# Four sums moved to GpSimd, second value products in halves, and a new order of sums and value copies in a fused attention and SwiGLU kernel

## The chip, the core and the metric

The kernel runs as one program on one core of a Trainium2 chip. The metric is the device time of one execution in microseconds (us); less is better. The times given are medians of runs.

## What is computed

Softmax attention for 8 batches of 12 heads, 448 tokens each, head size 64. Its output, seen as 3584 tokens of width 768, goes through a gated feed-forward network of inner width 1536:

```python
scores = matmul(q, k.transpose(0, 1, 3, 2)) / sqrt(64)
attn = exp(scores - max(scores)); attn = attn / (sum(attn) + 1e-09)
x = matmul(attn, v).transpose(0, 2, 1, 3).reshape(3584, 768)
g = x @ w_gate                                   # 768 -> 1536
out = (g * sigmoid(g) * (x @ w_val)) @ w_out     # 1536 -> 768
```

All inputs and the output are float32; the kernel works on float16 copies and accumulates in float32.

## The kernel before, in words

**Attention.** Two heads make a pair; there are 48 pairs, numbered 0 to 47. A pair's scores come from `qk` (lines 327, 339, 357), ScalarE takes their exponentials into `E` (lines 347, 365), and the product with the values accumulates in `acc` (lines 383, 391, 418). VectorE closes a pair with a reciprocal and a multiplication (lines 402 and 404 for the first twelve pairs, 447 and 448 for the others) into `xt`, which is then transposed into `X`, the input of the feed-forward part (lines 483 and 490 by TensorE and VectorE, 492 and 496 by DMA). Before a pair's value product can start, VectorE copies its values from the landing place `vraw` to `vo` (`copy_v`, line 218). The loads into `vraw` are issued by GpSimd (lines 177, 211). For the first six pairs the list `CAT` says behind which score unit each copy stands in VectorE's queue: entry 2 is pair 2, entry 3 is pair 3. `XAT` does the same for the transposes.

**Feed-forward, first half.** Every two batches (896 tokens) are cut into two blocks; a *block* of 384 or 512 tokens is worked off in 12 *steps*, one for each 128 of the 1536 inner columns. A step has a gate product (`gate`, tile `gp`), a tanh on ScalarE (`sg`, line 582), `t = (sg + 1) * gp` on VectorE (`gated`, line 608), a value product (`value`, tile `vp`) and `hts = t * vp` on VectorE (`close`, line 614). Both products are six matmuls of line 555. `run_pair` runs two steps together: gate one, gate two, value one, value two. Where a step has `split`, its value product is made in two halves of the tokens, each followed by its own `close`; the first half goes to `spare`, the unused second bank of the first step's gate tile. In the kernel before, the second step of a pair is split when the block is 512 tokens wide and the pair is not in a place marked `gate_small`.

**PSUM.** The pool `ps_s` has three tiles of two banks (scores, gates, the groups `og`, the units `un`), the pool `ps_f` two tiles of one bank (`acc`, `vp`, `op`, `ub`). A tile's next user waits until the last reader of the former one is done.

**Feed-forward, second half.** Part of it is plain (`op`, line 648, 12 matmuls of 192 columns). The rest goes by `out_group` (line 677), which needs seven products instead of eight for two blocks of 128 tokens, and for that needs sums made beforehand: `out_sums` (lines 527 to 530) over the weights, and `h_sums` (lines 538 to 541) over `hts`: `s3 = a11 - a21`, then `a21 = a21 + a22` in place, `s2 = a21 - a11`, `s4 = a12 - s2`. All of these are VectorE instructions on 128x768 float16. They wait in the list `sums`; `add_sum` issues the next one.

**Order.** The order of the instructions of each engine is the order of the calls. The list `VISITS` says for each visit of the main loop how many steps, groups, plain outputs and sums are issued; its last number is the number of sums. `FIRST_STEPS` does so for the seven visits before it. In the last three visits block 4 (384 tokens), the last in-line block, is waiting for its output groups; its four `h_sums` are issued there.

**The end.** After the loop, block 5 (512 tokens in two halves of 256) is made by `Unit`: 12 units of seven products (`un`, `ub`, line 793) between which ScalarE and VectorE combine (lines 835, 839, 842, 846, 858, 860). Units 0 and 1 begin with a small matmul `Z` (line 830) into a bank of `ps_f`. The units need sums of the weights, made by GpSimd (`weight_sums`, lines 756 to 759, four instructions of 128x384 float16 each; `W_6` to `W_11` in the list of items). `order_of` plans the order of all items from costs given by hand. Behind the units come one plain output (`O`), block 4's groups, block 5's groups, then the last block in the same way with 448 tokens.

Of the kernel before, what the change touches and what calls it, by code (L numbers as in the profile page):

```python
# [38 lines left out]
PE_, ACT_, DVE_, POOL_ = "PE", "ACT", "DVE", "POOL"  # L39
# [25 lines left out]
def kernel(  # L65
# [10 lines left out]
    nc = tc.nc  # L76
# [6 lines left out]
    NFB = DF // 128  # L83
# [66 lines left out]
    def hview(lo, n):  # L150
        return hall[:, ds(lo * NFB, n * NFB)].rearrange("p (f t) -> p f t", t=n)
# [64 lines left out]
    def copy_v(pr):  # L216
        m = 128 if pr >= QUAD else P
        nc.vector.tensor_copy(Vts[pr % NV][0:m, :, :, 0:D], vraw[0:m, pr % VS])
# [299 lines left out]
    gate_small = [False]  # L518
# [11 lines left out]
            lambda: nc.vector.tensor_sub(t4, b21, t2),  # L530
        ]

    def h_sums(hts, t, at):
        lo, hi, x, y = slice(0, NH), slice(NH, NFB), ts(2 * t, 128), ts(2 * t + 1, 128)
        a11, a12, a21, a22 = hts[:, lo, x], hts[:, hi, x], hts[:, lo, y], hts[:, hi, y]
        s2, s3, s4 = Hall[at]
        return [
            lambda: nc.vector.tensor_sub(s3, a11, a21),
            lambda: nc.vector.tensor_add(a21, a21, a22),
            lambda: nc.vector.tensor_sub(s2, a21, a11),  # L540
            lambda: nc.vector.tensor_sub(s4, a12, s2),
        ]

    class Step:
# [337 lines left out]
    with tc.manual_schedule():  # L882
# [33 lines left out]
        def emit(item):  # L916
            if item[0] == "qk":
                load_qk16(*item[1:])
            elif item[0] == "V":
                load_v(item[1] * GP, GP)  # L920
            else:
                load_w(*item)
# [8 lines left out]
        sums = []  # L931
# [14 lines left out]
        def add_block(i, visits):  # L946
            if i < B - NB - 1:
                f1, own, n = block(i)
                fvq.extend(f1)
                kk, c0, hts = own  # L950
            else:
                own = None
            t_out = NFB * OH / 2400.0
            if i == 0:
                oq.extend([(ffn2_steps(*own, by_half(range(n // 128), OH)), t_out)] * (2 * (n // 128)))
            if i < 2:
                if i:
                    ffn2_wait.append(own)
                    sums.extend(wsums)
                    wsums.clear()  # L960
                return
            kk, c0, hts = ffn2_wait.pop()
            ffn2_wait.append(own)
            odd = i % 2 == 0
            groups.extend(x for t in range(1 + odd) for x in pair_groups(kk, c0, hts, t))
            if not odd:
                w = QW
                oq.extend([(ffn2_steps(kk, c0, hts, by_half([2], w)), t_out)] * (DM // w))
            sums.extend(groups[0][1])
            later = [f for _, fs in groups[1:] for f in fs]  # L970
            groups[:] = [(begin, []) for begin, _ in groups]
            sums.extend(later)
# [11 lines left out]
        ]  # L984

        def token_sums(x, w, t, eng=nc.vector):
# [22 lines left out]
        def add_sum(n=1):  # L1009
            for _ in range(n):  # L1010
                if sums:
                    sums.pop(0)()

        def run_fv(quiet=False):
            step = fvq.pop(0)
            step.gate()
            step.value(0)
            if not quiet:
                add_sum()
            step.finish()  # L1020
            if not quiet:
                add_sum()
            return 2 * step.time

        def run_pair(small=0):
            one, two = fvq.pop(0), fvq.pop(0)
            two.split = two.at[2] == 512 and not gate_small[0]
            one.gate()
            two.gate()
            two.spare = one.spare  # L1030
            one.value(0)
            one.gated()
            if small == 1:
                add_sum()
            two.gated()
            one.finish()
            two.value(0)
            if not small:
                add_sum()
            two.finish()  # L1040
            if small == 2:
                add_sum()
            return 4 * one.time

        def run_single():
# [14 lines left out]
        def run_o():  # L1060
            gen, t = oq.pop(0)
            next(gen)
            if len(oq) < 2 and not groups and wsums:
                n = 3 if oq else 4
                sums.extend(wsums[:n])
                wsums[:n] = []
                add_sum(n)
            return t
# [38 lines left out]
        def run_budget(budget):  # L1107
            while (fvq or oq) and budget > 0:
                if not fvq:
                    budget -= run_o()  # L1110
                elif len(fvq) > 1 and fvq[0].at[1] and 2 * fvq[0].time < budget <= 4 * fvq[0].time:
                    budget -= run_pair(2)
                else:
                    budget -= run_fv(bool(fvq[0].at[1]))
            return budget

        def left():
            return sum(2 * step.time for step in fvq) + sum(t for _, t in oq)
# [2 lines left out]
            return (at + 1) * total // n - at * total // n  # L1121

        XAT = (10, 14, 17, 21)
        CAT = (3, 7, 11, 14, 17, 21)
        pieces = [(p, c) for p in range(FIRST) for c in range(NC)]

        def piece():
# [2 lines left out]
        for u in range(FIRST * NC):  # L1130
# [12 lines left out]
            if c == 1:  # L1143
                for w in wq.pop(pr, []):
                    emit(w)
            if u in CAT:
                copy_v(CAT.index(u))
            if u in XAT:
# [42 lines left out]
        def bare_next(x):  # L1191
            return x + 1 < len(plan) and not plan[x + 1][1]
# [9 lines left out]
        for x, (chunks, todo) in enumerate(plan):  # L1202
# [54 lines left out]
            if 0 < base - x <= len(FIRST_STEPS):  # L1257
                n = FIRST_STEPS[x - base]
                gate_small[0] = bare
                if n > 1:  # L1260
                    run_pair(1)
                else:
                    run_fv(True)
            elif x < base:
                if bare and oq and not fvq:
                    carry -= run_o()
                elif bare:
                    gate_small[0] = True
                out_small[0] = not fvq and bool(oq) and any(p0 >= QUAD for _, p0 in todo)
                extra = 2 * fvq[0].time if bare and len(chunks) == 3 and fvq and not fvq[0].at[1] else 0  # L1270
                carry = run_budget(left() / (end - x) + carry + extra) - extra
            else:
                begins, nf, ng, no, ns = VISITS[x - base]
                gate_small[0] = bare
                if begins > 2:
                    add_block(begins, 0)
                after_group = ng > 0
                out_small[0] = bool(no) and not bare
                if around:
                    run_group_with(todo[0][1])  # L1280
                elif ng:
                    run_group(nf, gate_first=bare)
                    nf = 0
                if bare_next(x):
                    for _ in range(nf):
                        run_fv()
                else:
                    run_steps(nf)
                for _ in range(no):
                    run_o()  # L1290
                    out_small[0] = True
                out_small[0] = False
                if begins == 2:
                    add_block(2, 0)
                ahead = {3: (x + 1, x + 2), 2: (), 1: ()}.get(len(VISITS) + base - x, (x + 1,))
                for p0 in [p for y in ahead for p in vcopies.get(y, [])]:
                    copy_v(p0)
                add_sum(ns)
                if x == len(VISITS) + base - 6:
                    space = raws_all[:, 0 : RL // 2].rearrange("p a t b x -> p (a t b x)")  # L1300
                    wsum_space(space, 10)
                    for _ in range(3):
                        wsum_space(attp.tile([128, 4 * NC * D], FP16, tag="qk16", name="wsum", bufs=3), 2)
                    wsum_space(Eall, 4)
                    wsum_space(vfree, 4)
# [60 lines left out]
        items = unit_items(units, lambda u: Unit(u, 256, x5, t5, hts5), 256)  # L1366
# [13 lines left out]
        for m, fn in enumerate(groups5[0][0][1]):  # L1380
            u = NFB - 1 if m else NH - 1
            items[f"H{m}"] = (DVE_, 0.6, [f"F00_{u}", f"F10_{u}"] + [f"H{m - 1}"] * (m > 0), fn)

        items["O"] = (PE_, 1.0, [f"P{n}_{NFB - 1}" for n in (2, 3, 4)], run_o)
        run_items(items)

# [18 lines left out]
        hts = hview(0, NT)  # L1405
        units = {}
        items = unit_items(units, lambda u: Unit(u, S, x7, t7, hts), S)
# [51 lines left out]
```

## Time and profile before

| | |
|---|---|
| median of 3 runs | 436.31 us (435.48 to 436.58) |
| profiled execution | 436.53 us, of it 434.8 us span |
| TensorE (PE) busy | 423.5 us, 97% of the span |
| VectorE (DVE) busy | 272.4 us, 63% |
| ScalarE (ACT) busy | 245.5 us, 56% |
| GpSimd (POOL) busy | 226.7 us, 52% |
| granted TensorE clock | 1.0 of full speed, throughout |

"PE s L327" is the TensorE instruction of line 327 that writes the tile `s`. In the timeline each row has the start in us, the time from the first start to the last end, the engine, the line, output and inputs, shapes and number of instructions; what stands in brackets is how long the engine had been idle before, and what ended that. Ends of matmuls are modelled: consecutive rows of PE overlap by the length of the pipeline, so distances between starts tell more than busy times. "PEld" is the weight load in front of a matmul.

### The profile page before, as it was taken

What the parts mean: (1) busy time and instruction counts of PE and PEld (TensorE: products, weight loads), DVE (VectorE), ACT (ScalarE), POOL (GpSimd) and SP (SyncE); (2) the same over time, 40 slices, a digit from 0 to 9 for tenths busy, and PEclk for the clock granted to TensorE, in tenths of its full rate; (3) what the DMA queues carried; (4) which work ended last, traced back from release to release, by engine and by line L of the source; (5) the groups of instructions that cost most, each with busy time, mean ns of one, the idle gap of its engine ahead of it and who ended that gap; (6) DMA issues with size and microseconds to landing.
All of it is one profiled execution on the core that took longest, in us unless ns stands there. A gap on an engine that the chain in (4) does not pass through costs nothing.

```text
span 434.8 us, 11461 instructions
## 1 busy us (share of the span) xinstructions
PE 423.5 (97%) x4564; PEld 284.5 (65%) x4564; DVE 272.4 (63%) x634; ACT 245.5 (56%) x395; POOL 226.7 (52%) x350
## 2 busy tenths in 40 slices
PE   8999999999999999999999999999899999999996
PEld 3665666645456667747665677776688995555795
DVE  4666652785668556565635776678777655575663
ACT  6875667646656655656666546668454225545221
POOL 8755723998795774647743875926992000000001
PEclk9999999999999999999999999999999999999999
DMA  9999999999999999999889999623100322000124
GB/s 133 191 199 200 198 168 177 137 170 218 141 132 144 117 165 116 133 137 125 117 127 134 166 125 100 138 54 95 23 2 3 110 83 64 0 2 0 38 75 146
DMA packets 108550, 50.01 MB, mean 115 GB/s; under 512 B 60864, under 2 KB 105232, under 8 KB 108496
## 3 DMA queue, kind: packets, MB, share of 16 engines
q0 software_dynamic: 46944, 24.83, 52.0%
q1 hardware_dynamic: 61408, 24.27, 31.0%
q8 instruction: 36, 0.59, 0.6%
q14 instruction: 18, 0.15, 0.2%
q10 hardware_dynamic: 144, 0.17, 0.1%
HBM read 49.55 MB, written 11.01 MB: 139 GB/s over the span
## 4 chain that ended last, share of the span: by engine, by line
PE 85%; DVE 9%; ACT 3%; issue 2%; DVEq 0%
PE og L677 17%; PE gp L555 14%; PE vp L555 12%; PE un L793 9%; PE ub L793 7%; PE acc L418 7%; PE s L327 4%; PE op L648 3%; PE s L357 2%; PE acc L383 2%; DVE hts L614 2%; DVE t L608 1%; PE tp L300 1%; ACT E L347 1%; PE wp L163 1%
## 5 line engine op out<-in xcount | busy, mean ns | idle before, releaser
L347 ACT ACTIVATE E<-s 128x896 f16<-128x896 f32 x126 | 106.6, 919 | 40.3 <-PE s L327 28.3
L237 POOL COPY qk<-qkraw 128x512 f16<-128x512 f16 x72 | 43.3, 646 | 59.8 <-DMA qkT<-qk 58.7
L555 PE MATMUL gp<-X,wg 128*128 128x384 f16 (+1 forms) x360 | 73.9, 347 | 0.0
L555 PE MATMUL vp<-X,wv 128*128 128x384 f16 (+2 forms) x360 | 71.6, 338 | 0.2
L608 DVE SCALAR_TENSOR_TENSOR t<-sg,gp 128x384 f32<-128x384 f32 (+1 forms) x60 | 36.3, 606 | 42.3 <-ACT sg L582 42.1
L555 PEld LDWEIGHTS <-wv 128*128 128x128 f16 x390 | 38.0, 98 | 29.4 <-issue 0.6
L638 POOL DMA_DIRECT2D out_dram<-osb x3 | 1.6, 539 | 100.3 <-ACT osb L696 100.3
L555 PEld LDWEIGHTS <-wg 128*128 128x128 f16 x360 | 32.8, 98 | 26.2 <-issue 1.9
L582 ACT ACTIVATE sg<-gp 128x384 f32<-128x384 f32 (+1 forms) x60 | 32.0, 536 | 30.8 <-PE gp L555 30.1
L177 POOL DMA_DIRECT2D vraw<-in_v_dram x72 | 44.2, 640 | 9.3 <-DVE R L402 7.4
L177 POOL DMA_DIRECT2D qkraw<-in_k_dram x70 | 42.7, 630 | 6.6 <-DMA wo<-in_moe_w_out_dram 5.8
L418 PEld LDWEIGHTS <-E 128*128 128x128 f16 (+1 forms) x1152 | 37.4, 96 | 13.3 <-issue 8.1
L365 ACT ACTIVATE E<-s 112x896 f16<-112x896 f32 x48 | 40.4, 923 | 8.8 <-PE s L357 8.6
L418 PE MATMUL acc<-vo,E 128*128 128x65 f16 (+1 forms) x1152 | 44.1, 193 | 1.1 <-DVE hts L614 0.4
L677 PEld LDWEIGHTS <-hts 128*128 128x128 f16 x528 | 44.1, 98 | 1.0 <-issue 0.8
L614 DVE SCALAR_TENSOR_TENSOR hts<-t,vp 128x384 f16<-128x384 f32 (+2 forms) x60 | 35.0, 584 | 6.3 <-PE vp L555 2.9
L696 ACT ACTIVATE osb<-og 128x384 f32<-128x384 f32 x22 | 10.8, 490 | 40.1 <-PE og L677 36.4
L200 POOL DMA_DIRECT2D qkraw<-in_q_dram x44 | 30.2, 685 | 3.8 <-PE vp L555 1.6
L448 DVE TENSOR_TENSOR xt<-acc,R 128x256 f16<-128x256 f32 x72 | 30.6, 424 | 2.5
L327 PE MATMUL s<-qkT 64*128 64x448 f16 x216 | 30.0, 354 | 0.7 <-DVE hts L614 0.6
L677 PE MATMUL og<-wo,hts 128*128 128x192 f16 x264 | 29.0, 246 | 0.0
L677 PEld LDWEIGHTS <-hsum 128*128 128x128 f16 x300 | 25.6, 98 | 1.0
(176 smaller groups left out, 712.4 us busy)
## 6 DMA issues: line engine op xcount, KB each, us to landing
vraw<-in_v_dram POOLq DMA_DIRECT2D x72, 64.0 KB, 4.8
qkraw<-in_q_dram POOLq DMA_DIRECT2D x41, 112.0 KB, 4.3
qkraw<-in_k_dram POOLq DMA_DIRECT2D x68, 64.0 KB, 4.8
wg<-in_moe_w_gate_dram POOLq DMA_DIRECT2D x8, 288.0 KB, 9.7
wv<-in_moe_w_val_dram POOLq DMA_DIRECT2D x8, 288.0 KB, 10.3
wo<-in_moe_w_out_dram POOLq DMA_DIRECT2D x2, 1152.0 KB, 19.7
out_dram<-osb SPq DMA_DIRECT2D x7, 288.0 KB, 3.9
out_dram<-osb SPq DMA_DIRECT2D x6, 336.0 KB, 3.6
```

The source lines that it names most:

```text
L177: eng.dma_start(dst[ts(s, 64)], rows)
L237: nc.gpsimd.tensor_copy(dst.rearrange("p c h d -> p h c d"), src)
L327: nc.tensor.matmul(s[:, hx, 0:S], lhsT=t[ts(hx, 64), ts(c + low(pr, hx), 128)], rhs=t[ts(hx, 64), ds(NC * 128, S)], start=True, stop=True,)
L347: nc.scalar.activation(e[:, 0 : 2 * S].rearrange("p (h q) -> p h q", h=2), s[:, :, 0:S], AF.Exp, scale=sm_scale)
L365: nc.scalar.activation(e[:, :, 0:S], s[0:P, :, 0:S], AF.Exp, scale=sm_scale)
L418: nc.tensor.matmul(acc[:, ts(j, D + 1)], lhsT=e[rows, ds(hx * S + j * 128, 128)], rhs=Vts[pr % NV][rows, hx, col, 0 : D + 1], start=first, ...
L555: nc.tensor.matmul(dst[:, 0:w], lhsT=wslice(kind, self.fb, cb), rhs=X[kk][:, cb, ds(c0 + lo, w)], start=(cb == 0), stop=(cb == NCB - 1),)
L582: self.readers = [nc.scalar.activation(self.sg[:, 0:n], gp[:, 0:n], AF.Tanh, scale=0.5)]
L608: nc.vector.scalar_tensor_tensor(self.t1[:, 0:n], self.sg[:, 0:n], 1.0, self.gp[:, 0:n], ALU.add, ALU.mult)
L614: nc.vector.scalar_tensor_tensor(self.hts[:, self.fb, ds(lo, w)], self.t1[:, ds(lo, w)], 0.5 * HS, vp[:, 0:w], ALU.mult, ALU.mult)
L677: nc.tensor.matmul(dst, lhsT=lhs(n), rhs=rhs(n), start=first and n == 0, stop=n == NH - 1, skip_group_check=True)
L793: mm = nc.tensor.matmul(dst, lhsT=lhs[:, n], rhs=rhs[:, n], start=first and n == 0, stop=n == NK - 1, skip_group_check=True,)
```

## The change

1. `h_sums` takes the engine as an argument. Block 4's four sums are no longer issued in the last three visits on VectorE (their counts in `VISITS` become 0 and the list is cleared); they become four items `G0` to `G3` on GpSimd behind `W_11`, in the part with block 5's units.
2. `run_pair` splits the second value product for 384 tokens as well (two halves of 192 columns).
3. `run_pair` issues its one sum always behind the second step. Before, it stood behind the first step's `gated` in the visits of `FIRST_STEPS` (argument 1), between the second step's two halves in the visits of `VISITS` (0), or behind the pair (2).
4. `CAT` issues the value copies of pairs 2 and 3 behind score units 9 and 13 instead of 11 and 14.

```diff
-    def h_sums(hts, t, at):
+    def h_sums(hts, t, at, eng=nc.vector):
...
-            lambda: nc.vector.tensor_sub(s3, a11, a21),
-            lambda: nc.vector.tensor_add(a21, a21, a22),
-            lambda: nc.vector.tensor_sub(s2, a21, a11),
-            lambda: nc.vector.tensor_sub(s4, a12, s2),
+            lambda: eng.tensor_sub(s3, a11, a21),
+            lambda: eng.tensor_add(a21, a21, a22),
+            lambda: eng.tensor_sub(s2, a21, a11),
+            lambda: eng.tensor_sub(s4, a12, s2),
...
-            (5, 0, 0, 1, 1), (0, 0, 0, 2, 2), (0, 0, 0, 0, 1),
+            (5, 0, 0, 1, 0), (0, 0, 0, 2, 0), (0, 0, 0, 0, 0),
...
-        def run_pair(small=0):
+        def run_pair():
             one, two = fvq.pop(0), fvq.pop(0)
-            two.split = two.at[2] == 512 and not gate_small[0]
+            two.split = not gate_small[0]
             one.gate()
             two.gate()
             two.spare = one.spare
             one.value(0)
             one.gated()
-            if small == 1:
-                add_sum()
             two.gated()
             one.finish()
             two.value(0)
-            if not small:
-                add_sum()
             two.finish()
-            if small == 2:
-                add_sum()
+            add_sum()
             return 4 * one.time
...
-                    budget -= run_pair(2)
+                    budget -= run_pair()
...
-        CAT = (3, 7, 11, 14, 17, 21)
+        CAT = (3, 7, 9, 13, 17, 21)
...
-                    run_pair(1)
+                    run_pair()
...
+        sums.clear()
+        for m, fn in enumerate(h_sums(hview(0, 384), 0, 0, nc.gpsimd)):
+            items[f"G{m}"] = (POOL_, 1.85, [f"G{m - 1}" if m else f"W_{NFB - 1}"], fn)
         items["O"] = (PE_, 1.0, [f"P{n}_{NFB - 1}" for n in (2, 3, 4)], run_o)
```

## The prediction

> **What bounds the kernel now.** I read the page's busy times, then who made TensorE wait (the view of waits), then the timelines of the engines around each wait.
>
> ```profile
> PE 423.5 (97%) x4564; PEld 284.5 (65%) x4564; DVE 272.4 (63%) x634; ACT 245.5 (56%) x395; POOL 226.7 (52%) x350
> ```
>
> TensorE sets the time. The change removes no matmul, so it can only gain what TensorE waits. All waits listed come to 5.5 us; the five largest:
>
> ```profile
> PE ub L830 <- DVE xt L448: 1.2, 1, 1.2
> PE wp L163 <- DVE warm L884: 1.0, 1, 1.0
> PE ub L793 <- DVE un L842: 0.9, 1, 0.9
> PE acc L383 <- DVE X L490: 0.6, 1, 0.6
> PE s L327 <- DVE hts L614: 0.6, 1, 0.6
> ```
>
> The change aims at four of them (not at the 1.0 at the start). Each has VectorE work queued ahead of what TensorE needs. These waits run from a modelled matmul end; distances between starts add some tenths.
>
> **Part 1, block 4's sums to GpSimd.** VectorE as the units begin:
>
> ```profile
> 300.01 1.26 DVE L538 TENSOR_TENSOR hsum<-hts 128x768 f16<-128x768 f16 x1
> 301.20 1.27 DVE L993 TENSOR_TENSOR vraw<-X,vraw 128x768 f16<-128x768 f16 x1
> 302.39 1.26 DVE L539 TENSOR_TENSOR hts<-hts 128x768 f16<-128x768 f16 x1
> 303.69 1.15 DVE L540 TENSOR_TENSOR hsum<-hts 128x768 f16<-128x768 f16 x1
> ...
> 305.85 1.04 DVE L541 TENSOR_TENSOR hsum<-hts,hsum 128x768 f16<-128x768 f16 x1
> ```
>
> The four sums hold VectorE 1.26 + 1.26 + 1.15 + 1.04 = 4.7 us, while GpSimd makes weight sums. Behind them stand the closes of pairs 46 and 47. TensorE needs their bank:
>
> ```profile
> 303.74 0.49 PE L793 MATMUL un<-X,wg 128*128 128x256 f16 x3
> 305.44 0.28 PE L830 MATMUL ub<-X,ident 128*128 128x256 f16 x1 [1.21 <-DVE xt L448]
> ```
>
> Without the sums VectorE is free at 301.4. Pair 46's product ends near 302.7 and its two closes (0.17 + 0.42, twice, overlapping) end by 304.0; pair 47's by 305.1. Line 830 then follows the three matmuls directly, at 304.07 instead of 305.44: 1.37 us. What is late next? ScalarE has its table at 304.0; its two copies (0.37, 0.38) end at 305.05, line 842 starts at 305.4 instead of 307.91, and line 793, which waited for it till 308.38, starts at 305.95, when TensorE gets there by its own work. Together **2.4 us** (1.37 plus a 1.07 gap).
>
> The sums now run on GpSimd. Its nearest rows, and a sum of the same shape on VectorE after GpSimd has finished:
>
> ```profile
> 309.36 0.91 POOL L756 TENSOR_TENSOR E<-wv 128x384 f16<-128x384 f16 x1
> ```
> ```profile
> 335.82 0.56 DVE L539 TENSOR_TENSOR hts<-hts 128x768 f16<-128x768 f16 x1
> ```
>
> Twice the elements: at most 2 x 0.91 = 1.82 us each when alone. The last weight sum ends at 328.5, and about 1.0 earlier with less VectorE traffic against it (five of GpSimd's rows between 300.8 and 307.7 took 1.1 to 1.2 instead of 0.91). The sums then end at 329.3, 331.2, 333.0, 334.8. Block 4's first group, at 335.96 before, moves to 333.5; its second product needs the second sum at 334.0, its third the third sum at 334.5, its sixth the fourth at 337.5. All are in time.
>
> But VectorE's own three sums for block 5 (0.56 each from 335.82, now from 333.4) are now beside GpSimd's third and fourth. By the 1.26 above they take about 1.2 while that lasts. The group's lines 719 and 721 queue behind them: line 721 ended at 338.34, 0.6 before the product that waits for it; it becomes 0.4 to 0.8 late, and line 725, behind the 0.85 us line 990, may add 0.4. I take 0.8 off, bounds 0 and 1.3. Part 1 is **1.6 us** (1.1 to 2.4).
>
> Beside each other both engines' instructions lengthen at once in the rows: VectorE's 1.26 for 0.56 and GpSimd's 1.22 (at 303.20) for 0.91. The Trainium skill (SBUF — State Buffer, "Summary: rules for kernel authors") says instead that a VectorE instruction with two SBUF inputs and a GpSimd instruction that reads SBUF block each other fully, the later one until the other has finished. By that the first of VectorE's three sums would stand until GpSimd's fourth is over, and part 1 would be near 1.2 instead of 1.6.
>
> **Part 2, halves for 384 columns.** Six pairs are affected (gates at 132.2, 144.2, 157.3, 170.2, 242.7, 248.3). Each makes 12 matmuls of 192 instead of 6 of 384: 24 matmuls of `og` with 192 columns take 1.98 us in the chain (82.5 ns each), 6 of 384 take 0.97, so 0.99 against 0.97, 0.1 us in all. VectorE makes two closes instead of one: 0.36 each by line 719's row, against 0.56, beside TensorE. The gain: the last close starts at the same time and is 0.2 shorter, and the next pair's second accumulation waits for its bank:
>
> ```profile
> 161.90 1.25 PE L418 MATMUL acc<-vo,E 64*128 64x65 f16 x32
> ...
> 241.72 1.12 PE L418 MATMUL acc<-vo,E 64*128 64x65 f16 x32
> ```
>
> The first follows an unsplit pair, the second a split one. The excess over 1.12 behind the six pairs is 0.12, 0.21, 0.13, 0.13, 0 and 0.13; and in the second pair the value product itself takes 2.31 instead of 2.11, waiting for a bank that the first half no longer needs. Sum 0.9. Against it: 0.1 of matmuls, and `spare` keeps the first step's gate tile until the first half is closed, which the next score may meet in the second pair (0.1). Part 2: **0.6 us** (0 to 0.9).
>
> **Part 3, the sum behind the pair.** It matters in the first of the `FIRST_STEPS` pairs:
>
> ```profile
> 89.59 1.54 DVE L530 TENSOR_TENSOR qkraw<-wo,E 128x768 f16<-128x768 f16 x1
> 91.05 0.68 DVE L608 SCALAR_TENSOR_TENSOR t<-sg,gp 128x512 f32<-128x512 f32 x1
> ```
>
> This sum lies before the second step's line 608, and three line 614 behind that. Two scores wait for gate tiles; the accumulation starts 1.59 us after the first score (91.31 to 92.90) where 0.58 is usual (99.28 to 99.86). With the sum last, line 608 starts at 89.6, the closes end at 91.2 and 91.8, and nothing waits: 1.0, and 0.14 more of a late second bank (1.26 for 1.12). The sum then runs from 91.8 to 93.3, and pair 14's closes stand behind it: half a microsecond late, with 2.6 us of gates before the next value product wants their banks. In the pair at 127 another 0.14 goes. In the others the sum lay in VectorE's idle time; there it moves behind the pair, ahead of the next close, with 0.6 of idle time to take it, and the group sums keep 0.6 before their products. Part 3: **1.2 us** (0.8 to 1.3).
>
> **Part 4, values of pairs 2 and 3.** Only VectorE's two copies move, ahead of casts and copies for TensorE; no DMA and no other queue does. Pair 2's load is issued at 8.54 and such loads take 4.9 (median), so it lands at 13.4; VectorE is idle from 13.9 to 15.2. Pair 3's must have landed by 19.44, where the copy ran without a wait; its new place is 17.1. Of the two 336 KB loads, with median 8.8, the longer took 11.7 and was the later one, so this took 5.9 and landed at 16.6. The two copies (0.52, 0.56) leave the way of line 490; the waits at 16.83 and 20.51 (0.2, 0.6) go: 0.8 us. I do not carry it on, because of this:
>
> ```profile
> 77.06 0.67 DVE L218 COPY vo<-vraw 128x512 f16<-128x512 f16 x1 [0.73 <-DMA vraw<-in_v_dram]
> ```
>
> Pair 12's values land at 77.0, issued at 63.4 and 65.4 behind the output weights, whose landing GpSimd waits for until 74.64; the DMA engines are full from 4 us on. Line 490 stands behind this copy, and the accumulation at 78.07 needs both. TensorE would come there 0.8 earlier and wait. Part 4: **0.1 us** (0 to 0.8; if a load came late, the copy would hold VectorE, but this wait would take that up too).
>
> **Sum.** 1.6 + 0.6 + 1.2 + 0.1 = 3.5 us. Behind 78 us I find no other wait for a load that a shift could meet. The profiled execution had 436.53 us (434.8 span and 1.7 around it), so 433.0; the median is 0.22 lower: 436.31 - 3.5 = **432.8 us**.
>
> **The rivals.**
> *The start's gain carries on.* If pair 12's load lands earlier because GpSimd's issue at 63.39 waited for VectorE (6.8 us), part 4 gives 0.8: 432.1. For it: that wait. Against: the next issue waited for another DMA. Chance 0.19.
> *The groups take back part 1.* The second sum writes `hts` in place and may be held until the last plain output, also a reader of `hts`, has ended at 333.5. Then it ends at 335.4 and the third at 337.3, where products wanted them at 334.0 and 334.5: 2.8 late, plus 0.4. Part 1 is -0.8, the sum 1.1: 435.2. Nothing in the trace shows such a hold. Chance 0.13.
> *Slower: GpSimd's sums are too slow.* If beside VectorE they lengthen as VectorE's do (1.26 / 0.56 = 2.25), each takes 4.1: the fourth ends at 327.5 + 16.4 = 343.9 instead of 337.5, 6.4 late. Part 1 is -4.0, the sum -2.1: 438.4. It turns to a loss from 3.6 us per sum on. Against: GpSimd's slowest such row is 1.23, and most of VectorE's unit work reads PSUM and left GpSimd at 0.91. Chance 0.07.
> *The copies and sums move, but ScalarE binds the units' start.* The table load ends at 304.0, and I have counted it; no chance of its own.
>
> **How the numbers follow.** My forecast has 0.61. With the bounds of parts 1 to 3 it spans 431.6 to 434.4; the range reaches down for the first rival and up over the second: 431.3 to 435.4. About 0.3% (1.3 us) can be told from no change: faster is below 435.0. The forecast and the first rival give faster 0.81; the second, just above, most of same 0.12; the third slower 0.07.
>
> **What would show it.** Right: the waits of lines 830 and 793 (842) gone, the units' first `ub` some 0.3 behind their first `un`; `hsum` by GpSimd near 1.8 us; the accumulations behind 384 pairs at 1.12; no wait of line 327 near 92; at 77 a longer wait for pair 12's values. Wrong: a wait of `og` for GpSimd, sums above 2.5 us, or 0.8 us of lead still there behind 80 us.

## The result, and the profile after

| | before | after |
|---|---|---|
| median of 5 runs each | 436.03 us | 433.53 us (433.07 to 433.79) |
| ratio, 95% interval | | 0.994 (0.9925 to 0.9954) |
| profiled execution | 436.53 us, span 434.8 | 433.57 us, span 431.8 |

The change makes the kernel 2.5 us faster by the medians and 2.96 us by the profiled executions. Part by part the two traces are compared by TensorE's *lead*: the start of one instruction before, minus the start of the same instruction after. A lead of 0.22 us has built up by 6.3 us, ahead of everything that the change touches, and is no effect of it.

The page's busy times of the changed kernel:

```profile
PE 422.4 (98%) x4594; PEld 286.4 (66%) x4594; DVE 270.3 (63%) x635; ACT 245.5 (57%) x395; POOL 233.6 (54%) x354
```

GpSimd has four instructions and 6.9 us more, TensorE 30 matmuls more, which is five pairs of six and not six.

The waits of TensorE for other engines, changed kernel (us in total, times, longest):

```profile
PE wp L163 <- DVE warm L884: 1.0, 1, 1.0
PE acc L418 <- DVE hts L614: 0.4, 2, 0.2
PE ub L793 <- DVE un L842: 0.4, 1, 0.4
PE tp L278 <- DVE qk L257: 0.3, 1, 0.3
PE s L357 <- DVE qkT L286: 0.3, 1, 0.3
PE acc L418 <- DVE X L490: 0.3, 1, 0.3
PE og L677 <- DVE og L721: 0.2, 1, 0.2
PE ub L793 <- DVE kept L846: 0.2, 1, 0.2
PE og L677 <- DVE osb L725: 0.2, 1, 0.2
```

Of the waits of before, 1.2 (line 830), 0.9 (line 793 for 842 at the units' start) and the two of 0.6 (line 327, and line 383 at 20.5 us) are gone. New are 0.3 of `tp` at the start, 0.3 of line 418 for line 490 at 78 us, the 0.4 of line 793 and the two of `og`. Line 793's and the one for line 721 stand behind the units' start, the one for line 725 at 141 us. TensorE's timeline of the changed kernel shows the gain and where these waits are:

```profile
90.88 0.74 PE L327 MATMUL s<-qkT 64*128 64x448 f16 x6
91.46 1.12 PE L418 MATMUL acc<-vo,E 64*128 64x65 f16 x32
...
141.28 0.66 PE L677 MATMUL og<-qkraw,hts 128*128 128x192 f16 x6 [0.16 <-DVE osb L725]
...
301.86 0.49 PE L793 MATMUL un<-X,wg 128*128 128x256 f16 x3
302.18 0.27 PE L830 MATMUL ub<-X,ident 128*128 128x256 f16 x1
...
328.26 0.49 PE L793 MATMUL ub<-vraw,wsum 128*128 128x256 f16 x3 [0.36 <-DVE un L842]
...
335.65 0.67 PE L677 MATMUL og<-E,hsum 128*128 128x192 f16 x6 [0.21 <-DVE og L721]
```

In the first two lines the accumulation follows the scores after 0.58 us, where it took 1.59 before, and lasts 1.12. At 302 us the small matmul of line 830 starts 0.32 behind the unit's first product, as forecast; before it was 1.70. The lead over the whole kernel:

| place (us, before) | lead | what it shows |
|---|---|---|
| 16.8, 20.5 | 0.50, 0.97 | part 4 |
| 78.3 | 0.40 | wait for pair 12's values |
| 93.0 | 1.58 | part 3 |
| 131.2 | 1.71 | part 3, the pair near 127 |
| 136.9 | 1.82 | part 2, first pair |
| 142.7 | 1.46 | lost: a group's wait for line 725 |
| 253.0 | 1.88 | part 2, the other pairs |
| 305.4, 308.4 | 3.26, 4.34 | part 1 |
| 331.9, 338.9, 340.4 | 3.65, 3.29, 3.02 | units, block 4's groups |
| end of span | 3.0 | |

The 0.36 us lost at 142.7 are not lost in a second trace of the same kernel. They begin on VectorE some microseconds earlier, where two sums are long:

```profile
134.85 0.64 DVE L538 TENSOR_TENSOR hsum<-hts 128x768 f16<-128x768 f16 x1
135.52 0.85 DVE L539 TENSOR_TENSOR hts<-hts 128x768 f16<-128x768 f16 x1
```

In the second trace they take 0.55 and 0.56. GpSimd works on two copies (line 237) from 134.47 to 135.97 here, and the second sum ends 0.40 behind them. Of the fourteen traces of this document, five have two sums of 0.64 to 1.00 at this place, and these five have TensorE's wait for line 725; the nine others have neither.

Part 1 wins 2.46 us at the units' start and loses 1.32 again before the end. The loss is seen on VectorE and GpSimd. VectorE's timeline, changed kernel:

```profile
325.82 1.38 DVE L860 SCALAR_TENSOR_TENSOR hts<-silu,kept 128x256 f16<-128x256 f32 x1
327.12 0.41 DVE L860 SCALAR_TENSOR_TENSOR hts<-silu,un 128x256 f16<-128x256 f32 x1
...
331.05 1.37 DVE L860 SCALAR_TENSOR_TENSOR hts<-silu,kept 128x256 f16<-128x256 f32 x1
...
333.11 0.56 DVE L539 TENSOR_TENSOR hts<-hts 128x768 f16<-128x768 f16 x1
...
335.23 0.36 DVE L721 SCALAR_TENSOR_TENSOR og<-p,og 128x192 f32<-128x192 f32 x1
```

GpSimd's timeline, the same kernel:

```profile
325.28 1.64 POOL L538 TENSOR_TENSOR hsum<-hts 128x768 f16<-128x768 f16 x1
327.00 1.70 POOL L539 TENSOR_TENSOR hts<-hts 128x768 f16<-128x768 f16 x1
328.78 1.64 POOL L540 TENSOR_TENSOR hsum<-hts 128x768 f16<-128x768 f16 x1
330.50 1.64 POOL L541 TENSOR_TENSOR hsum<-hts,hsum 128x768 f16<-128x768 f16 x1
```

Line 860 with two inputs in SBUF (`silu` and `kept`) starts 0.54 us into GpSimd's first sum (325.28 to 326.92) and ends at 327.20; the second starts 0.55 into the fourth (330.50 to 332.14) and ends at 332.42. Both end 0.28 behind the end of the sum. I call that a *hold*. The same line with one input in PSUM (`un`) takes 0.41 at 327.12 beside GpSimd's second sum. VectorE's own sum at 333.11, which the forecast feared for, comes after the last GpSimd sum and takes its usual 0.56. From 331.05 on VectorE has no pause until line 721 ends at 335.59, and at 335.65 TensorE has waited 0.21 for that line.

### The profile page after: what moved, and what is told of

The parts are those of the page before. It is cut to its first block, busy times and chain, and to the rows that moved or that the text cites. A ratio compares the mean times of both kernels' runs of the same rounds, so it can differ in the third digit from the quotient of the medians.

```text
span 431.8 us, 11525 instructions
## 1 busy us (share of the span) xinstructions
PE 422.4 (98%) x4594; PEld 286.4 (66%) x4594; DVE 270.3 (63%) x635; ACT 245.5 (57%) x395; POOL 233.6 (54%) x354
## 4 chain that ended last, share of the span: by engine, by line
PE 84%; DVE 7%; DMA 3%; ACT 3%; issue 1%; POOL 1%; SPq 0%; DVEq 0%; POOLq 0%
PE og L677 16%; PE gp L555 15%; PE vp L555 12%; PE un L793 9%; PE acc L418 7%; PE ub L793 7%; PE s L327 4%; PE op L648 3%; PE s L357 2%; PE acc L383 2%; DVE hts L614 2%; DMA qkT<-qk 1%; PE tp L300 1%; DVE t L608 1%; ACT E L347 1%
## 5 line engine op out<-in xcount | busy, mean ns | idle before, releaser
L237 POOL COPY qk<-qkraw 128x512 f16<-128x512 f16 x72 | 44.5, 659 | 55.8 <-DMA qkT<-qk 54.4
L555 PE MATMUL vp<-X,wv 128*128 128x384 f16 (+3 forms) x360 | 70.1, 332 | 0.2
L555 PEld LDWEIGHTS <-wv 128*128 128x128 f16 x420 | 40.3, 98 | 28.1 <-issue 0.6
L614 DVE SCALAR_TENSOR_TENSOR hts<-t,vp 128x384 f16<-128x384 f32 (+3 forms) x60 | 34.1, 568 | 7.2 <-PE vp L555 3.3
```

The source lines that it names most:

```text
L237: nc.gpsimd.tensor_copy(dst.rearrange("p c h d -> p h c d"), src)
L555: nc.tensor.matmul(dst[:, 0:w], lhsT=wslice(kind, self.fb, cb), rhs=X[kk][:, cb, ds(c0 + lo, w)], start=(cb == 0), stop=(cb == NCB - 1),)
L614: nc.vector.scalar_tensor_tensor(self.hts[:, self.fb, ds(lo, w)], self.t1[:, ds(lo, w)], 0.5 * HS, vp[:, 0:w], ALU.mult, ALU.mult)
```

## Experiments

Each kernel was run in several rounds beside the kernel before, whose medians were 435.74, 435.70 and 435.91 us in the three groups. Ratios are to it.

### Each part alone

Four kernels make one part of the change each, on the kernel before. `p1_gpsimd_sums` has the diff's `h_sums`, the zeros in `VISITS` and the items `G0` to `G3`; `p3_late_sum` the one `add_sum()` behind the pair; the other two are one line each:

```diff
# p2_halves
-            two.split = two.at[2] == 512 and not gate_small[0]
+            two.split = not gate_small[0]
# p4_copies
-        CAT = (3, 7, 11, 14, 17, 21)
+        CAT = (3, 7, 9, 13, 17, 21)
```

> Part 1 alone. Theory: the two waits of the units' start go (2.4 us), and GpSimd's 1.64 us sums take some back by holding VectorE's line 860 with two SBUF inputs (about 1.3 us in the trace of the changed kernel): net 1.0 to 1.3 us faster, about 435.0 where the kernel before has 436.1. Rival (the prediction's term): 1.6 us net, 434.4. A second rival: the whole gain of 2.4, if what is taken back comes from the other parts of the change.

> Part 2 alone: the second value product of the 384-token pairs in halves. Prediction's term: 0.6 us faster (0 to 0.9). Theory after reading the changed kernel's trace: only five pairs are split (30 more matmuls), the pair at 144 is not, and 0.1 us is won behind four of them: 0.3 us, within what a measurement can tell. Rival: without the late sum the halves win nothing, since the sum between them stands in front of the second close: 0.0.

> Part 3 alone: the sum of a pair always behind it. Prediction's term 1.2 us faster (0.8 to 1.3), nearly all of it at the first 512-token pair near 92 us, whose first accumulation follows its first score by 0.58 us again. Theory after the trace: 1.2 at 92 to 131, less 0.25 at the group near 142, where VectorE comes late to line 725: 1.0 us. Rival: the 1.54 us of the sum was a disturbance of that one execution, and in others part 3 wins 0.3.

> Part 4 alone: the copies of pairs 2 and 3 sooner. Theory: TensorE leads the kernel before by 0.8 us from 20 us on, and loses it all at the accumulation near 78 us, which waits for pair 12's values: 0.0 to 0.2 us faster at the end. Rival: the lead stays, 0.8 us faster.

| | median | ratio (95%) | won |
|---|---|---|---|
| part 1 alone | 435.11 | 0.9987 (0.9973 to 1.0002) | 0.6 |
| part 2 alone | 436.36 | 1.0011 (0.9999 to 1.0022) | -0.5 |
| part 3 alone | 435.47 | 0.9993 (0.9985 to 1.0002) | 0.3 |
| part 4 alone | 435.89 | 1.0015 (1.0001 to 1.0029) | -0.7 |

By these times parts 1 and 3 win less than their theories said (0.6 for 1.0 to 1.3, and 0.3, the rival's figure, for 1.0), and parts 2 and 4 do worse than either of their readings. The four sum to -0.3 us where the whole change won 2.5. Each interval is 0.4 to 0.7 us to either side, so the sum carries about 1 us of error. The single traces do not show that the parts need each other: TensorE's last matmul leads by 1.10, -0.07, 1.50 and 0.52 us, 3.05 in sum, where the whole leads by 3.02. All are measured from one trace of the kernel before, whose execution took 436.53 us, where that kernel's median beside these four was 435.74, so these leads are rather high. I cannot reconcile the two further.

*Part 1* does in its trace what it does in the whole: lead -0.09 at 253 us, 2.37 at the units, 1.10 at the end.

*Part 2* alone wins at two of its pairs and not at the others. TensorE and then VectorE in `p2_halves`:

```profile
161.94 1.12 PE L418 MATMUL acc<-vo,E 64*128 64x65 f16 x32
...
252.76 1.29 PE L418 MATMUL acc<-vo,E 64*128 64x65 f16 x32
```

```profile
252.07 0.55 DVE L540 TENSOR_TENSOR hsum<-hts 128x768 f16<-128x768 f16 x1
252.54 0.35 DVE L614 SCALAR_TENSOR_TENSOR hts<-t,vp 128x192 f16<-128x192 f32 x1
```

The accumulations at 161.94 and 174.65 fall from 1.25 to 1.12; no sum is issued in the pairs ahead of them. In the three other split pairs a sum stands between the two halves, so the second, shorter close is late all the same, and the accumulations take 1.28, 1.16 and 1.29, each 0.04 longer than before. Together with the unsplit pair (1.44 for 1.33) nothing is won. I had costed part 2 without that; at these three places it needs part 3.

*Part 3* alone moves the lead from -0.20 to 1.36 between 78 and 93 us; 0.4 of that lies at 85 us, ahead of the part's own place (below), so the part itself is near 1.2.

*Part 4* alone leads by 0.96 us at 20.5 us (0.21 of it from the start), loses 0.40 at 78 us and keeps the rest.

Why is the sum that part 3 moves so long in the kernel before? In `p2_halves` the sum keeps its old place, but starts a little earlier than GpSimd's two copies of line 237. VectorE and then GpSimd in `p2_halves`:

```profile
90.12 0.54 DVE L530 TENSOR_TENSOR qkraw<-wo,E 128x768 f16<-128x768 f16 x1
```

```profile
90.36 1.33 POOL L237 COPY qk<-qkraw 128x512 f16<-128x512 f16 x2
```

and GpSimd in the kernel before, where VectorE's sum started at 89.59 and took 1.54:

```profile
89.45 1.26 POOL L237 COPY qk<-qkraw 128x512 f16<-128x512 f16 x2
```

Started 0.14 behind the copies, the sum ends 0.42 behind their end at 90.71; started 0.24 ahead of them, it takes 0.54, the copies take 0.07 longer, and TensorE's line 327 does not wait there. Part 3 is worth 1.0 only while the sum meets the copies. In the kernels of part 1 alone, part 4 alone and all parts but the third the sum met them too (1.54, 1.46 and 1.55), so it did in four of the five traces that have the sum in its old place.

A start a little ahead is no safe place. In the same trace of `p2_halves` another sum starts 0.23 ahead of two copies and is held until 0.42 behind the second. VectorE and then GpSimd:

```profile
86.03 1.83 DVE L529 TENSOR_TENSOR E<-wo 128x768 f16<-128x768 f16 x1
```

```profile
86.26 1.19 POOL L237 COPY qk<-qkraw 128x512 f16<-128x512 f16 x2
```

In all fourteen traces 603 such sums (128x768, VectorE) are recorded. Of the 473 beside no copy or sum of GpSimd, 467 take at most 0.60 us. 109 take longer than 0.60; 95 of these end 0.40 to 0.43 behind the end of a copy or sum of GpSimd, and for the other 14 I have no cause.

### What gives back part 1

`a_no_gsums` leaves out the four sums, so that block 4's groups work on what happens to stand in their place; it is of use for its times alone.

```diff
# a_no_gsums: the changed kernel without block 4's four sums
-        for m, fn in enumerate(h_sums(hview(0, 384), 0, 0, nc.gpsimd)):
-            items[f"G{m}"] = (POOL_, 1.85, [f"G{m - 1}" if m else f"W_{NFB - 1}"], fn)
# a_half_gsums: each sum as two instructions of 128x384
-        for m, fn in enumerate(h_sums(hview(0, 384), 0, 0, nc.gpsimd)):
-            items[f"G{m}"] = (POOL_, 1.85, [f"G{m - 1}" if m else f"W_{NFB - 1}"], fn)
+        for m, fn in enumerate(h_sums_halves(hview(0, 384), 0, 0, nc.gpsimd)):
+            items[f"G{m}"] = (POOL_, 0.93, [f"G{m - 1}" if m else f"W_{NFB - 1}"], fn)
```

> The changed kernel once more, beside the others of this group. Theory: the parts add up with their spread, and the single parts summed to about 0.3 us slower to 0.5 us faster within 1 us of noise; the four together were 2.5 us faster. If the parts only add, this repeats at 1 to 2 us faster; if they help each other (late sum and halves, sums and copies), it repeats at 2.5.

> The changed kernel without block 4's four sums (their results are left out). Theory: with no GpSimd work behind the weight sums, line 860 stays near 0.7 us or below at 325 to 332 and the lead of the units' start is kept but for 0.2 us: 1.0 to 1.1 us faster than the changed kernel. Rival: the loss sits in the groups for another reason (their place among VectorE's sums for block 5), and at least 0.6 us of it stays.

> The changed kernel with each of GpSimd's four sums cut into two instructions of 128x384. Theory (one engine's whole instruction holds the other's two-input instruction): line 860 with both inputs in SBUF falls from 1.38 us to below 1.0 beside them, VectorE reaches its own three sums about 0.7 us sooner, and 0.4 to 0.8 us of the 1.3 that are lost between the units' start and the groups come back. Rival (both engines are slowed by a share): line 860 stays at 1.3 or more and nothing comes back; the eight instructions take 0.3 us more in all.

`a_again` is the changed kernel itself, in the same group: 433.31 us, ratio 0.9944 (0.9926 to 0.9962). `a_no_gsums`: 432.58, 0.9930 (0.9904 to 0.9956). `a_half_gsums`: 433.12, 0.9933 (0.9917 to 0.9949). These three cannot be told apart by their times, so `a_half_gsums`, the lowest of the kernels that do the whole work, is not shown to be better than the changed kernel; the traces can be told apart. VectorE in `a_no_gsums`:

```profile
325.92 0.42 DVE L860 SCALAR_TENSOR_TENSOR hts<-silu,kept 128x256 f16<-128x256 f32 x1
...
330.62 0.43 DVE L860 SCALAR_TENSOR_TENSOR hts<-silu,kept 128x256 f16<-128x256 f32 x1
```

and in `a_half_gsums`, where line 860 has become 876:

```profile
326.43 0.64 DVE L876 SCALAR_TENSOR_TENSOR hts<-silu,kept 128x256 f16<-128x256 f32 x1
...
331.13 0.47 DVE L876 SCALAR_TENSOR_TENSOR hts<-silu,kept 128x256 f16<-128x256 f32 x1
...
332.48 1.17 DVE L539 TENSOR_TENSOR hts<-hts 128x768 f16<-128x768 f16 x1
```

with GpSimd's last sum, in two halves:

```profile
331.27 1.97 POOL L556 TENSOR_TENSOR hsum<-hts,hsum 128x384 f16<-128x384 f16 x2
```

Without GpSimd's sums the two instructions take 0.42, and the lead over the changed kernel's own trace grows by 0.53 us up to 328, 0.90 up to 335 and 1.16 up to 337: all of the 1.32 but some 0.2. With sums half as long the hold is shorter, and 0.53 us is won up to 328 and 0.63 up to 336. Now VectorE's own first sum of block 5 is held (1.17 for 0.56) by GpSimd's last half, which ends at 333.24. What part 1 gives back is thus shown to come from GpSimd's sums. That the hold of line 860 is the way is shown for the first piece, at 328: the wait goes and comes with it. For the later pieces VectorE's rows without a pause from the second hold to line 721 say the same, and the wait for that line is gone from the lists of both kernels; I did not part the two holds by a run of their own. By the medians the two kernels are 0.7 and 0.2 us faster than the changed one, where 1.0 to 1.1 and 0.4 to 0.8 were expected.

### The wait for pair 12's values

```diff
# a_v12_early: the changed kernel with this load issued behind the second output-weight load
-            8: [("o", 1)],
+            8: [("o", 1), ("v1", 12)],
...
-                if 12 <= pr + 3 < NPAIR:
+                if 13 <= pr + 3 < NPAIR:
```

> The changed kernel with pair 12's values loaded directly behind the second half of the output weights, ahead of pair 14's keys and queries. Theory (the lead of the earlier copies dies at pair 12's values): they land 0.8 us or more before 77, the wait near 77 goes, and TensorE keeps 0.7 us more lead at 80 us; at the end 0.3 to 0.7 us faster than the changed kernel, less if pair 15's keys, now later, are waited for at 85. Rival: the lead is lost at 78 for another reason (the cast of line 490), and it is lost again.

Measured 434.2 us, 0.9957 (0.9940 to 0.9974), no better than the changed kernel, where 0.3 to 0.7 us less were expected. VectorE and then TensorE in this kernel:

```profile
75.85 0.48 DVE L218 COPY vo<-vraw 128x512 f16<-128x512 f16 x1
```

```profile
85.45 0.38 PE L339 MATMUL s<-qkT 64*64 64x448 f16 x3 [0.97 <-DMA qkT<-qk]
```

The copy no longer waits for the load; in the changed kernel it does:

```profile
76.90 0.43 DVE L218 COPY vo<-vraw 128x512 f16<-128x512 f16 x1 [1.52 <-DMA vraw<-in_v_dram]
```

So far the theory holds: from 20 to 80 us the trace gains 0.5 us on the changed kernel's. But TensorE then waits 0.97 us at 85 us for the transposed keys of pair 15 (GpSimd's copies end at 83.3, the second transpose is issued at 83.73). This wait comes and goes from kernel to kernel, between nothing and 0.97 us, also in kernels whose work up to there is the same, so one trace does not show whether the earlier load made it longer here. It stands ahead of parts 1 to 3 and blurs every comparison of whole times: the accumulation behind it starts anywhere from 84.52 to 86.27. So I also give the span behind that start.

### The change without each part

```diff
# wo_p1: the sums in VISITS again, no G items
# wo_p2
-            two.split = not gate_small[0]
+            two.split = two.at[2] == 512 and not gate_small[0]
# wo_p3: run_pair(small) with the sum in its three old places
# wo_p4
-        CAT = (3, 7, 9, 13, 17, 21)
+        CAT = (3, 7, 11, 14, 17, 21)
```

> The changed kernel without part 1 (block 4's sums on VectorE in the loop again). The changed kernel is 2.5 us faster than before. Theory: part 1 is worth 1.1 us (2.45 won at the units' start, 1.3 given back): 1.3 to 1.5 us faster than before, and both waits of the units' start are back. Rival: part 1 is worth the 0.6 us that it gave alone: 1.9 us faster.

> The changed kernel without part 2 (384-token pairs unsplit). Theory: four accumulations take 1.25 instead of 1.12 us again, 0.45 us lost: 2.0 us faster than before. Rival from the run of part 2 alone, which was 0.5 us slower: without it 3.0 us faster.

> The changed kernel without part 3 (each sum where it was). Theory: the wait near 92 us is back wherever the sum there is stretched, up to 1.2 us lost, and the halves of part 2 have their sum in front of the second close again, 0.3 us lost: 1.0 to 1.5 us faster than before. Rival from part 3 alone (0.3 us): 2.2 us faster.

> The changed kernel without part 4 (copies of pairs 2 and 3 as before). Theory: the lead of 0.8 us at 20 us is missing and the same lead as with it is there from 78 us on: 2.4 to 2.5 us faster than before. Rival: part 4 carries 0.8 us to the end: 1.7 us. Second rival, from part 4 alone (0.6 us slower): 3.1 us.

The worth of a part is its ratio minus 0.9944 (all parts, `a_again`, run in another group), times 435.9 us. From the two intervals of each difference it carries an error of about 1 us. "Behind 85" is the span behind the accumulation named above, one trace each: 346.9 and 346.3 for the two traces of the changed kernel, 349.5 before.

| without | median | ratio (95%) | worth of the part | behind 85 |
|---|---|---|---|---|
| part 1 | 435.02 | 0.9973 (0.9961 to 0.9984) | 1.3 | 348.7 |
| part 2 | 434.71 | 0.9968 (0.9953 to 0.9982) | 1.0 | 347.8 |
| part 3 | 434.53 | 0.9963 (0.9949 to 0.9977) | 0.8 | 348.3 |
| part 4 | 433.66 | 0.9942 (0.9925 to 0.9959) | -0.1 | 347.3 |

Now they sum to 3.0 us. Against the kernel before, these four are 1.2, 1.4, 1.6 and 2.5 us faster; 1.3 to 1.5, 2.0, 1.0 to 1.5 and 2.4 to 2.5 were expected. Parts 2 and 3 seem to be worth 1.8 together in company and -0.2 alone, but with these errors that is not shown. What the traces show of it is the three pairs above, where the halves need the sum out of the way. TensorE's waits in `wo_p1`:

```profile
PE ub L830 <- DVE xt L448: 1.2, 1, 1.2
PE wp L163 <- DVE warm L884: 1.0, 1, 1.0
PE ub L793 <- DVE un L842: 0.9, 1, 0.9
```

and in `wo_p3`:

```profile
PE s L327 <- DVE hts L614: 0.6, 1, 0.6
```

Without parts 1 and 3 their own waits of before come back, in the same size. In `wo_p2` TensorE's accumulations behind 384 pairs are long again:

```profile
161.83 1.25 PE L418 MATMUL acc<-vo,E 64*128 64x65 f16 x32
```

Against the changed kernel `wo_p2` loses 0.9 us behind 85. Of these, 0.6 lie at the four accumulations and the scores before the first of them. The other 0.3, near 139 us, come with GpSimd's copies: two of VectorE's sums ahead of that place take 0.91 and 0.85 beside them.

## Why the prediction was right or wrong

**Part 4 (0.1 forecast).** Right in mechanism, and not contradicted in size: 0.75 us was won by 20.5 us, and most of it (0.57) lost at 78 to the load; `wo_p4` ran at 433.66, like the changed kernel. Alone, the part kept 0.3 us in its trace and was 0.7 us slower by its ratio. One number was off: pair 3's values landed near 17.6 and not at 16.6, so the copy stood 0.58 us at VectorE's head. The rival "the start's gain carries on" fell: the load let the copy start at 76.90 for 77.06, no earlier than the lead of the start. With its wait taken away TensorE waited for pair 15's keys. My sentence that there was no other wait for a load behind 78 us failed there.

**Part 3 (1.2 forecast).** Right in size by the traces: 1.2 between 78 and 93 us in the changed kernel's lead and 0.1 at 131; 0.8 by the leave-out, 0.3 alone. What I had not seen is that the 1.54 us of the sum were a hold by GpSimd's copies, so the gain hangs on a few tenths of a microsecond between two queues of the kernel before.

**Part 2 (0.6 forecast).** By the lead 0.45 (0.11 or 0.12 behind each of four pairs), by the leave-out 1.0 (0.6 in the trace). The terms of the forecast, 0.9 less 0.1 and 0.1, come to 0.7 and not 0.6. The step that failed is the count: the pair at 144 us is marked `gate_small` and is not split (its value product stays at 2.31, the accumulation behind it at 1.25), so its 0.2 and 0.13 were never there to win. The others did as forecast, 1.25 to 1.12. With a sum between the halves a pair wins nothing, which the forecast did not ask.

**Part 1 (1.6 forecast).** The gain at the units' start was right: 2.46 for 2.4, with each of the two waits gone. GpSimd's sums took 1.64 to 1.70 for at most 1.82, and ended at 332.1 for 334.8, in time for every group. What was given back was 1.32 for 0.8, at the upper bound, and its mechanism was wrong. I took VectorE's three sums at 333 us to lengthen beside GpSimd; they met nothing, as GpSimd was done 2.7 us sooner than forecast. Held instead were the units' lines 860, which I had not costed. My text had set the units aside with "most of VectorE's unit work reads PSUM"; line 860 on `kept` does not. The net is 1.14 by the lead and 1.3 by the leave-out.

The reading of "both lengthen at once" failed with it. A row of 1.26 for 0.56 beside a GpSimd row of 1.22 for 0.91 is as well one waiting for the other in turn. In the kernel before, VectorE's sum of 1.26 us ends at 301.28, 0.42 behind a GpSimd sum that ended at 300.86, and it is the next GpSimd sum, started at 300.83, that takes 1.22. The rule of the Trainium skill (SBUF — State Buffer, "Summary: rules for kernel authors"), that the later of two such instructions stands until the earlier is over, agrees with three rows here: 1.38 and 1.37 beside sums of 1.64, and 1.17 beside a last half. Two rows do not fit it as it stands: the 1.54 behind two copies lasted past the first of them, and the 1.83 belongs to a sum whose row starts ahead of the copies. The 1.2 that I worked out from the rule for part 1 was nearer than my 1.6, but by luck, as it came through other instructions.

**Sum.** Forecast 3.5, measured 2.5 by the medians and 2.96 by the traces. Part 1 came 0.3 to 0.5 short, and the missing sixth pair takes up to 0.3. The changed kernel's trace also lost 0.36 at a group near 142 us, which the forecast did not count and a second trace does not have. The rival "groups take back part 1" gave 435.2 where 433.5 was measured, and its hold on `hts` did not occur: GpSimd's second sum started at 327.00, straight behind the first. The slower rival fell with 1.64 us per sum, where it needed 3.6. What stays open is the last half microsecond: the wait at 85 us varies by more than that, and the worth of a single part by leave-out carries an error of about 1 us.

## What to carry to other kernels

Moving work from VectorE to GpSimd does not only ask whether GpSimd has time: list every VectorE instruction with two SBUF inputs that will run beside it, and charge each with up to the whole length of the GpSimd instruction; shorter GpSimd instructions made shorter holds here. A VectorE row that is two or three times its usual length is worth a look at what GpSimd was doing, since a shift of a tenth or two can remove it or bring it back. Parts of a change that share a queue are to be tested by leaving each out of the whole, not only alone: alone, the halves won at two of their five places. And parts of a microsecond or less are to be read in the traces, place by place, and in more than one trace: here the whole times summed to -0.3 us for the parts alone and to 3.0 in company, each with an error of 1 us or more.

## What the runs showed of the hardware

A float32 `scalar_tensor_tensor` of 128x256 with both inputs in SBUF took 0.42 us beside an idle GpSimd and 1.38 when issued 0.54 us into a 1.64 us GpSimd sum: it ended 0.28 us behind it. The same instruction with one input in PSUM took 0.41 beside such a sum. A float16 sum of 128x768 near two GpSimd copies that follow each other was held for both in some rows (1.54 for 0.55) and got in between in others: 0.64 at 134.85, where the two copies took 1.50 us together for 1.19 elsewhere. Cutting GpSimd's 1.64 us sum in two cost 0.1 to 0.3 us a sum (1.77 to 1.97 for the pair of halves) and brought line 860 down from 1.38 and 1.37 to 0.64 and 0.47, but held another instruction (1.17 for 0.56): 0.9 us lost on VectorE in sum, where it was 1.9.
